# Delta rule with key products up to 15 chunks ahead, solved matrices through DRAM, and two moved pieces of work in the experts

## The chip, the cores and the metric

The kernel runs on one NeuronCore of a Trainium2 chip. Its five engines work side by side, each through its own instruction stream: PE (TensorE, matmuls; its weight loads are listed as PEld), DVE (VectorE), ACT (ScalarE), POOL (GpSimd) and SP (SyncE, which here only issues DMAs). The metric is the device time of one execution in microseconds (us), smaller is better. Before the change the median of three runs is 974.29 us (973.56 to 976.66).

## The reference

Three stages, one after the other, all in float32:

```
# 1. attention by the delta rule; q, k, v: [4 batches, 8 heads, 768 tokens, 48]
k_n = k / (norm(k) + 1e-06);  state = 0                       # 48 x 48 per head
for t in range(768):
    y[t]   = q[t] @ state
    v_old  = state applied to k_n[t]
    state += beta[t] * outer(k_n[t], v[t] - v_old)
# 2. mixture of experts: 3072 tokens of width 384, 8 experts, the best one each
e   = argmax(cosine(x, expert_emb) / tau)
out = gate * (relu(x @ w1[e]) @ w2[e])                         # 384 -> 1024 -> 384
# 3. dense feed-forward
h = relu(x @ w_in);  out = (h * h) @ w_out                     # 384 -> 2048 -> 384
```

## The kernel before

**The delta stage.** The 768 tokens are cut into 24 chunks of 32, and four chunks make a group (6 groups). Within a chunk the recurrence is turned into matrices, so that only the 48 x 48 states pass from chunk to chunk. For each chunk `gram` (lines 146 to 190) multiplies keys by keys and queries by keys (64 matmuls, line 154) and ACT copies the products to `GPs` and `Pm`. After the last chunk of a group from group 2 on, the products go to DRAM and come back laid out by lane: `GPs` to `gscr` (L176) and back as `AL` (L179), `Pm` to `pscr` (L184) and back as `PL2` (L188; `PL` in the rows). All four are DMAs that SP issues in order, so each waits for the one ahead of it.

`lanes` (lines 196 to 296) makes the list of DVE operations that solves a group's 128 triangular 32 x 32 systems at once, one per lane: 31 steps of a multiply into `tmp` (L269) and an add into `TL` (L277), with the scaling of `vV` (L259) and the masking of `PL` (L194) among the last steps. At the end four transposes on DVE (L282, `STREAM_TRANSPOSE`) turn the solved matrix `TL` into `TTt`, which PE reads in `W` (L343).

**The chunk loop** (from line 774) runs for each chunk: `mmV` and `mm1K` (PE, L301 and L313), `U` (L324 on DVE writes `Ub` from the PSUM tile `ch`), `W` (PE, L343, reads `Ub` and `TTt`; DVE and ACT then write `Wb`), one `gram` for a chunk further on, the router's logits of the chunk before (`xlog`), the state update `dS` (L362) and the output `PW` (L394). So from chunk to chunk DVE waits for PE at `Ub`, and PE waits for DVE at `W`. Which `gram` runs is set by `ahead` and its limit `min(15 if s < 4 else NS, s + 12)`: chunks 1 to 12 each run one of the grams 12 to 23.

**The planner.** The solving operations stand in streams, one per group, and `fill(now, part)` pops them into DVE's program three times per chunk: a cost in us is attached to each (`0.1 + n / 960`), `need` works out the pace at which every group would be done at its due time `due(g) = 4 * g` (the chunk of its first use), and `fill` pops as much as the pace allows. The order is fixed when the kernel is built; nothing of it is decided on the chip.

**The experts** (`moe`) run eight times: 8 blocks of the first product (line 1121 and on, tiles `gp`, `sp`, `yp`, `xp`; `hh` and `hl` are the high and the low part of the activation), and then the second product. The leftover 64 rows of an expert use `ht` (L1184, tile `t2k`), which DVE writes after the last block and PE waits for at L1208. Meanwhile DVE prepares the weights of stage 3: `w64` splits each of 28 pieces (lines 1058 to 1092) into parts that are stored to `wscr` and fetched back (L602). `run(k, ng, nw)` after each block pops `ng` gate operations and `nw` of these, two per block in the last expert. At the end PE places the last rows with one-hot matrices (`t2k` of L1245, matmuls of L926), POOL scatters rows into `x` in DRAM (L1216).

**The dense stage** is 8 blocks of 384 tokens, PE-bound. `load_x2(n + 1)` (lines 1130 to 1135) reads the rows of the next block from `x` and stands at the start of each block, the first included, ahead of some of the fetches of `W<-wscr` on SP.

Of the kernel before, what the change touches and what calls it, by code (L numbers as in the profile page):

```python
# [8 lines left out]
F32 = mybir.dt.float32  # L9
# [12 lines left out]
def kernel(  # L22
# [16 lines left out]
    nc = tc.nc  # L39
# [3 lines left out]
    NS, C = kq.shape[0], kq.shape[-1]  # L43
    S = NS * C
    E, _, FF = moe_w1.shape
# [13 lines left out]
    cp = pool("const")  # L59
# [3 lines left out]
    wscr = [dram.tile([128, 6144], F32, name=f"wscr{i}") for i in range(2)]  # L63
    pscr = [dram.tile([4, C, 4, 256], F32, name=f"pscr{i}") for i in range(2)]
    gscr = [dram.tile([4, C, C, C], F32, name=f"gscr{i}") for i in range(2)]

    ident = cp.tile([128, 128], F32, name="ident")
    magic = cp.tile([128, C], I32, name="magic")
# [40 lines left out]
    gp = apool("gp")  # L109
# [15 lines left out]

    def load_kq(s):
        if s % 3 == 0:
            KQ3[0] = cp.tile([128, 3, 4, 4, 2, C], F32, name="W", bufs=5)
        a = KQ3[0][:, s % 3]
        KQ[s] = a[:, :, :, 0], a[:, :, :, 1], a  # L130
        nc.sync.dma_start(a, kq[s])
# [14 lines left out]
    def gram(s, n0=0, n1=2, banks=GP2):  # L146

        g, i = divmod(s, 4)
        n = n1 - n0
        for p in range(4):  # L150
            for h2 in range(2):
                for b in range(4):
                    r = 64 * h2
                    PE.matmul(
                        banks[h2][C * b : C * b + C, p * n * C : (p + 1) * n * C],
                        KQ[s][0][r : r + 64, p, b],
                        KQ[s][n0][r : r + 64, p, b]
                        if n == 1
                        else KQ[s][2][r : r + 64, p, b].rearrange("d n j -> d (n j)"),
                        start=True,  # L160
                        stop=True,
                    )
        if i == 0 and n0 == 0:
            GPs[g] = gp.tile([128, 4, 8, C], F32, name="GPs", bufs=3)
        if i == 0 and n1 == 2:
            Pm[g] = gp.tile([128, 4, 4, 2, C], F32, name="Pm", bufs=3)
        for m in range(n0, n1):
            for h2 in range(2):
                if m == 0:
                    o = GPs[g][:, i].rearrange("p (x a c) j -> p c x a j", x=2, c=2)[:, h2]  # L170
                else:
                    o = Pm[g][:, :, i].rearrange("p (a c) x j -> p c x a j", c=2)[:, h2]
                src = banks[h2][:, : 128 * n].rearrange("p (x a n j) -> p n x a j", x=2, a=2, n=n)
                A.activation(o, src[:, m - n0], AF.Copy)
        if i == 3 and n0 == 0 and g > 1:
            nc.sync.dma_start(gscr[g % 2].rearrange("b i u j -> (b i) (u j)"), GPs[g].rearrange("p s h j -> p (s h j)"))  # L176
            ALs[g] = wp.tile([128, C, C], F32, name="AL", bufs=3)
            for b in range(4):
                nc.sync.dma_start(ALs[g][C * b : C * b + C], gscr[g % 2][b].rearrange("i u j -> u i j"))  # L179
        if i == 3 and n1 == 2:  # L180
            scr = pscr[g % 2]
            PL2[g] = gp.tile([128, 4, 4, 2, C], F32, name="PL2", bufs=4)
            for b in range(4):
                nc.sync.dma_start(  # L184
                    scr[:, :, b, :].rearrange("f j x -> j f x"),
                    Pm[g][C * b : C * b + C].rearrange("p f s c j -> p f (s c j)"),
                )
            nc.sync.dma_start(  # L188
                PL2[g].rearrange("p b s c j -> p (b s c j)"), scr.rearrange("f j b x -> (f j) (b x)")
            )  # L190
# [5 lines left out]
    def lanes(g):  # L196
# [82 lines left out]
        def end(i):  # L279
# [3 lines left out]
                TTl[g].rearrange("p u i -> p i u")[:, i : i + 8], T.rearrange("p c i -> p i c")[:, i : i + 8]  # L283
            )

        for j in range(31):
            for f in (mul, acc):
                add(lambda f=f, j=j: f(j), (31 - j) * (j + 1))
            if j in (23, 25, 27, 29):
                u = (j - 23) // 2  # L290
                add(lambda u=u: vh(u), 384)
                if g:
                    add(lambda u=u: masked(g, u), 256)
        for i in range(0, C, 8):
            add(lambda i=i: end(i), c=0.55)
        return ops

    def mmV(s, hq):

# [235 lines left out]
    def padding(e):  # L535

        o = xs[e * CAP : (e + 1) * CAP] if e < E else x2[0:384]
        n = 112 if e < E else 128
        nc.scalar.dma_start(
            o.rearrange("(a p) c -> p a c", p=n),  # L540
            pad[:n, : o.shape[1]].unsqueeze(1).broadcast_to([n, o.shape[0] // n, o.shape[1]]),
        )
# [96 lines left out]
        V.tensor_tensor(lo, raw1[a], hi.bitcast(F32), ALU.subtract)  # L639

    def attention():
        streams, route_q = deque(), deque()
        budget, lent = 0.0, 0.0

        class Stream:
# [6 lines left out]
            def pop(self):  # L652
                c, f = self.ops.popleft()
                f()
                self.left -= c
                if not self.ops:
                    streams.remove(self)
                return c

        def need(now):  # L660
# [33 lines left out]
                budget = 0.0  # L694

        def due(g):
            return 4 * g

        def queue(fs):
            route_q.extend(fs)  # L700
# [70 lines left out]
        for s in range(NS):  # L771
            g, i = divmod(s, 4)
            last = g == NG - 1
            while s not in ready:
                streams[0].pop()
            if s:
                mmV(s, 0)
                mmV(s, 1)
                mm1K(s, 0)
                mm1K(s, 1)  # L780
            U(s)
            fill(s, 0.25)
            if s:
                mm1Q(s)
            if s > 0:
                xT = xrt(s - 1)
            while streams and streams[0].g <= g:
                streams[0].pop()
            W(s, 0)
            W(s, 1)  # L790
            if s == NS - 1:
                lows.pop(0)()
            if s == 0:
                for b in range(4):
                    masked(0, b)
            if ahead < min(15 if s < 4 else NS, s + 12):
                gram(ahead)
                ahead += 1
            if scats and s >= E:
                drain(route_q)  # L800
                scats.pop(0)()
            fill(s + 0.25, 0.4)
            if s == NS - 4:
                first_x()
            if s >= NS - 3:
                pre1(s - NS + 3, False)
            if scats and s >= NS - 10:
                scats.pop(0)()
            if R is not None and s in (6, 10, 14, 17, 19):
                drain(route_q)  # L810
                R[1]()
                queue(R[2])
                scats += R[3]
            if s > 0:
                xlog(s - 1, xT)
                if i == 0 or s == 18:
                    R = route(g, 0, 2) if i else route(g - 1, 2 if s == 20 else 0, 4)
                    R[0][0]()
                    queue(R[0][1:])
                    if last and i == 0:  # L820
                        drain(route_q)
            if s + 1 < NS:
                dS(s, 0)
                dS(s, 1)
            if s == NS - 1:
                R = route(NG - 1, 2, 3)
                for o in R[0]:
                    o()
            PW(s)
            if last and i == 0:  # L830
                R[1]()
                queue(R[2])
                scats += R[3]
            if s <= E:
                padding(s)
            if i == 3 and g + 2 < NG:
                load_v(g + 2)
                load_k2(g + 2)
            if s % 3 == 2:
                for n in range(s + 13, min(s + 16, NS)):  # L840
                    load_kq(n)
            if ahead % 4 == 0 and ahead // 4 - 1 > made:
                made += 1
                streams.append(Stream(made, s + 1.6))
            fill(s + 0.65, 0.35)
            if s in (15, 17, 20):
                pre1((15, 17, 20).index(s), True)
            if s in (NS - 3, NS - 2):
                R = route(g, s - NS + 3, s - NS + 4)
                for o in R[0] + [R[1]] + R[2]:  # L850
                    o()
                scats += R[3]
# [241 lines left out]
    def moe():  # L1094
# [48 lines left out]
        for e in range(E):  # L1143
# [21 lines left out]
            for fb in range(8):  # L1165
# [11 lines left out]
                if fb == 3 and e + 1 < E:  # L1177
                    load_x(e + 1)
                if e:
                    run(fb + 1, 4, 2 if e + 1 == E else (1, 1, 0, 1, 0, 1, 0, 1)[fb])  # L1180
                else:
                    run(fb + 1, (0, 0, 0, 0, 2, 4, 6, 9)[fb], 1)
            ht = mp.tile([128, 8, 64], F32, name="t2k", bufs=2)
# [66 lines left out]
        for o in late:  # L1250
            o()
        for n in range(NBLK):
            if n + 1 < NBLK:
                load_x2(n + 1)
            xhn, xln = xh[f"a{n}"], xl[f"a{n}"]
            sh, sl = [
# [4 lines left out]
            for fb in range(16):  # L1261
# [13 lines left out]
                def part2(fb=fb, s2=s2, sh=sh, sl=sl):  # L1275
                    A.activation(sh[fb], s2, AF.Copy)
                    V.tensor_tensor(sl[fb], s2, sh[fb].bitcast(F32), ALU.subtract)

                if n == 0:
                    weights(10 * E + 2 + (fb + 1) * 8 // 15)  # L1280
            part2()
# [76 lines left out]
```

## Time and profile before

| | us |
|---|---|
| median of 3 runs | 974.29 (973.56 to 976.66) |
| the profiled execution | 973.39 |
| its span | 971.6 |
| PE busy in it | 908.7 (94%) |
| DVE busy in it | 620.7 (64%) |
| ACT busy in it | 443.6 (46%) |

The profile shows one execution. Start times count from the beginning of its span. The delta stage lies between 49 and 268 us, the first expert's start follows, the experts run to 556 us, the dense stage to the end. The mean clock that TensorE was granted over the span is 0.951 of the full one. A row of a timeline gives start, duration, engine, line, operation, the tile written and the tile read, a count, and in brackets the idle time before it with the instruction that ended it.

### The profile page before, as it was taken

The page shows a single profiled execution, that of the slowest core. Times are in us where ns is not written, and L with a number is a line of the kernel's source. Part 1 is how long each engine was busy: PE and PEld are TensorE (multiplying, and loading weights), DVE is VectorE, ACT ScalarE, POOL GpSimd, SP SyncE. Part 2 cuts the span into 40 slices and gives each one's busy share as a digit, 9 for nine tenths or more (in the row PEclk, how much of TensorE's full clock was granted, in tenths as well). Part 3 has the DMA queues.
Part 4 walks back from the last instruction along what each step waited for, and adds up shares of the span by engine and source line. Part 5 has one row for each costly group of instructions (what it writes and reads, how often), then busy time and mean ns, then how long its engine had stood idle before and what let it go on. Part 6 is the DMA issues. An engine that isn't in the chain of part 4 may idle for free. (4 is left out here: it accounts for less than half of the span.)

```text
span 971.6 us, 22202 instructions
## 1 busy us (share of the span) xinstructions
PE 908.7 (94%) x8982; PEld 810.4 (83%) x8982; DVE 620.7 (64%) x1641; ACT 443.6 (46%) x1051; POOL 89.4 (9%) x126
## 2 busy tenths in 40 slices
PE   4778889899999999999999899999999999999998
PEld 3456667677777798888887689999999999999998
DVE  7999997899667888888789572423334241516060
ACT  2247656557734555455555362423333242415150
POOL 2000012011211122212211200000000000000000
PEclk7579988789989999999999999999999999999999
DMA  8667865441145677477557450101010101010000
GB/s 322 204 186 230 251 172 191 102 144 58 65 142 187 214 245 243 133 245 252 175 181 241 147 163 17 33 9 42 9 41 9 41 9 41 1 49 1 25 1 25
DMA packets 70608, 117.75 MB, mean 121 GB/s; under 512 B 22659, under 2 KB 48746, under 8 KB 70496
## 3 DMA queue, kind: packets, MB, share of 16 engines
q1 hardware_dynamic: 60784, 94.08, 30.4%
q0 software_dynamic: 5440, 15.88, 4.3%
q10 hardware_dynamic: 4272, 6.28, 2.0%
q8 instruction: 72, 1.18, 0.5%
q14 instruction: 40, 0.33, 0.1%
HBM read 84.12 MB, written 32.89 MB: 120 GB/s over the span
## 5 line engine op out<-in xcount | busy, mean ns | idle before, releaser
L1272 DVE TENSOR_TENSOR t4k<-t2k 128x384 f32<-128x384 f32 x128 | 71.4, 558 | 231.9 <-ACT t2k L1271 231.3
L277 DVE TENSOR_TENSOR TL<-TL,tmp 128x31 f32<-128x31 f32 (+15 forms) x186 | 62.7, 340 | 3.6
L269 DVE TENSOR_TENSOR tmp<-AL,TL 128x31 f32<-128x31 f32 (+15 forms) x186 | 62.4, 339 | 3.3
L1121 PE MATMUL gp<-wb,hh 128*128 128x384 f32 x184 | 62.9, 342 | 0.0
L1123 PE MATMUL gp<-wb,hl 128*128 128x384 f32 x184 | 62.0, 337 | 0.6 <-DVE hl L1174 0.6
L1122 PE MATMUL gp<-wb,hh 128*128 128x384 f32 x184 | 61.8, 336 | 0.0
L372 ACT ACTIVATE Sb<-sp 48x384 f32<-48x384 f32 x92 | 44.6, 484 | 34.0 <-PE sp L362 32.5
L1121 PE MATMUL sp<-xh,W 128*128 128x384 f32 (+1 forms) x150 | 51.0, 340 | 2.2 <-ACT t2k L1271 2.2
L1122 PE MATMUL yp<-xl,W 128*128 128x384 f32 (+1 forms) x153 | 52.6, 344 | 0.1
L1121 PE MATMUL yp<-xh,W 128*128 128x384 f32 (+1 forms) x153 | 52.5, 343 | 0.2 <-ACT xh L950 0.2
L1123 PE MATMUL yp<-xh,W 128*128 128x384 f32 (+1 forms) x153 | 52.6, 344 | 0.0
L1123 PE MATMUL gp<-xh,W 128*128 128x384 f32 (+1 forms) x153 | 52.1, 340 | 0.0
L1121 PE MATMUL gp<-xh,W 128*128 128x384 f32 (+1 forms) x153 | 52.0, 340 | 0.0
L1122 PE MATMUL gp<-xl,W 128*128 128x384 f32 (+1 forms) x153 | 51.9, 340 | 0.0
L362 PE MATMUL sp<-Wb,kL 128*48 128x96 f32 x736 | 49.5, 291 | 2.3 <-issue 1.4
L1121 PE MATMUL xp<-wb,hh 128*128 128x384 f32 x152 | 51.3, 338 | 0.0
L1123 PE MATMUL sp<-xh,W 128*128 128x384 f32 (+1 forms) x150 | 51.2, 341 | 0.0
L1123 PE MATMUL xp<-wb,hl 128*128 128x384 f32 x152 | 51.1, 336 | 0.0
L1122 PE MATMUL xp<-wb,hh 128*128 128x384 f32 x152 | 51.1, 336 | 0.0
L1122 PE MATMUL sp<-xl,W 128*128 128x384 f32 (+1 forms) x150 | 50.9, 340 | 0.0
L1216 POOL DMA_INDIRECT x<-y,rows x32 | 35.4, 1105 | 127.2 <-ACT y L1213 72.6
L362 PEld LDWEIGHTS sp<-Wb,kL 128*48 128x48 f32 x736 | 41.7, 149 | 6.0 <-ACT Wb L356 2.6
(314 smaller groups left out, 2463.7 us busy)
## 6 DMA issues: line engine op xcount, KB each, us to landing
W<-in_moe_w_dram SPq DMA_DIRECT2D x42, 256.0 KB, 3.6
W<-in_kq_dram SPq DMA_DIRECT2D x20, 512.0 KB, 7.0
hb<-in_moe_w_dram SPq DMA_DIRECT2D x24, 384.0 KB, 3.3
t4k<-in_moe_w_in_dram SPq DMA_DIRECT2D x12, 512.0 KB, 4.2
t4k<-in_moe_w_out_dram SPq DMA_DIRECT2D x16, 384.0 KB, 3.7
W<-wscr SPq DMA_DIRECT2D x16, 384.0 KB, 4.1
xs<-padrow ACTq DMA_DIRECT2D x8, 693.0 KB, 5.1
xe<-xs SPq DMA_DIRECT2D x8, 594.0 KB, 8.3
```

What stands on the lines that cost most here:

```text
L269: V.tensor_tensor(tv[0], AL[:, j, j + 1 :].unsqueeze(1).broadcast_to([128, n, m]), T[:, :n, j : j + 1].broadcast_to([128, n, m]), ALU.mult,)
L277: V.tensor_tensor(T[:, : j + 1, j + 1 :], T[:, : j + 1, j + 1 :], tv[0], ALU.add)
L362: PE.matmul(SP_[hq][64 * par : 64 * par + D, b * 96 : b * 96 + 96], kL2[g][:, i, b * 2 + hq], Wb[hq].rearrange("p b (m r) e -> p b r m e", ...
L372: A.activation(Sb[hq][r : r + D, :, :, par, :], SP_[hq][r : r + D, 0:384].rearrange("p (b m e) -> p b m e", b=4, m=2), AF.Copy,)
L1121: PE.matmul(ps, hs, rh, start=first, stop=False)
L1122: PE.matmul(ps, hs, rl, start=False, stop=False)
L1123: PE.matmul(ps, ls, rh, start=False, stop=last)
L1216: to_x2 = lambda n=n, t=t, y=y, rows_e=rows_e: G.indirect_dma_start(out=x2, out_offset=bass.IndirectOffsetOnAxis(ap=rows_e[:n, t : t + 1]. ...
L1272: V.tensor_tensor(s2, r, r, ALU.mult)
```

## The change

- The solved matrices of groups 2 to 5 are no longer transposed on DVE. When such a group's stream ends, `stored` writes `TL` to a DRAM tile `tscr` (one DMA on SP), and `relaid` reads it back with rows and columns exchanged into `TTt` (four DMAs on SP). `relaid` is called at the end of a chunk, from chunk 4g - 5 on, or at the latest ahead of `W`.
- These groups are due at 4g - 2.2 instead of 4g.
- Two grams may run in a chunk from chunk 2 on, and the limit of `ahead` is 15, 18 or s + 15. The grams run in chunks 0 (12), 1 (13), 2 (14), 3 (15, 16), 4 (17, 18), 5 (19) and so on to 9 (23).
- The keys and queries of chunks 15 to 17 are loaded in chunk 0 into a buffer of their own, and each later load comes three chunks earlier; `GPs` and `Pm` have two buffers instead of three.
- In the last expert 2, 2, 2, 2, 2, 2, 0, 0 of the `w64` operations are popped after the eight blocks instead of two after each.
- `load_x2(1)` stands after the tenth of the 16 parts of dense block 0 instead of at its start.

```
+    tscr = [dram.tile([4, C, C, C], F32, name=f"tscr{i}") for i in range(2)]
...
-            KQ3[0] = cp.tile([128, 3, 4, 4, 2, C], F32, name="W", bufs=5)
+            KQ3[0] = (wp if s == 15 else cp).tile([128, 3, 4, 4, 2, C], F32, name="W", bufs=1 if s == 15 else 5)
...
-            GPs[g] = gp.tile([128, 4, 8, C], F32, name="GPs", bufs=3)
+            GPs[g] = gp.tile([128, 4, 8, C], F32, name="GPs", bufs=2)
...
+        def stored():
+            nc.sync.dma_start(tscr[g % 2].rearrange("b u c i -> (b u) (c i)"), T.rearrange("p c i -> p (c i)"))
...
-        for i in range(0, C, 8):
+        if g > 1:
+            ops.append((0.0, stored))
+        for i in range(0, C if g < 2 else 0, 8):
             add(lambda i=i: end(i), c=0.55)
         return ops
+
+    def relaid(g):
+
+        TTl[g] = wp.tile([128, C, C], F32, name="TTt", bufs=2)
+        for b in range(4):
+            nc.sync.dma_start(TTl[g][C * b : C * b + C], tscr[g % 2][b].rearrange("u c i -> c u i"))
...
         def due(g):
-            return 4 * g
+            return 4 * g - (2.2 if g > 1 else 0)
...
+            if g not in TTl:
+                solved.remove(g)
+                relaid(g)
             W(s, 0)
...
-            if ahead < min(15 if s < 4 else NS, s + 12):
-                gram(ahead)
-                ahead += 1
+            for _ in range(2 if s > 1 else 1):
+                if ahead < min(15 if s < 3 else 18 if s < 4 else NS, s + 15):
+                    gram(ahead)
+                    ahead += 1
...
+            if s == 0:
+                for n in range(15, 18):
+                    load_kq(n)
...
-                for n in range(s + 13, min(s + 16, NS)):
+                for n in range(s + 16, min(s + 19, NS)):
...
+            old = list(solved)
             fill(s + 0.65, 0.35)
+            for x in old:
+                if s >= 4 * x - 5:
+                    solved.remove(x)
+                    relaid(x)
...
-                    run(fb + 1, 4, 2 if e + 1 == E else (1, 1, 0, 1, 0, 1, 0, 1)[fb])
+                    run(fb + 1, 4, ((1, 1, 0, 1, 0, 1, 0, 1), (2, 2, 2, 2, 2, 2, 0, 0))[e + 1 == E][fb])
...
-            if n + 1 < NBLK:
+            if 0 < n < NBLK - 1:
                 load_x2(n + 1)
...
+                if n == 0 and fb == 9:
+                    load_x2(1)
```

Three places of the program show the moves. The first is SP, from the load of `vV` for group 2 on, before the change; the buffers' numbers tell neighbouring groups apart.

```order
L140 DMA vV<-in_v_dram 128x1536
L144 DMA kL_1602<-in_k_dram 128x1536
L176 DMA gscr_67<-GPs 128x1024
L179 DMA AL<-gscr_67 32x32x32 x4
L184 DMA pscr_65<-Pm 32x4x256 x4
L188 DMA PL_1719<-pscr_65 128x1024
L131 DMA W<-in_kq_dram 128x1024 x3
L140 DMA vV<-in_v_dram 128x1536
```

The same stretch of SP after the change (the old line numbers are up to 28 higher there).

```order
L177 DMA gscr_67<-GPs 128x1024
L180 DMA AL<-gscr_67 32x32x32 x4
L185 DMA pscr_65<-Pm 32x4x256 x4
L189 DMA PL_1603<-pscr_65 128x1024
L141 DMA vV<-in_v_dram 128x1536
L145 DMA kL_1695<-in_k_dram 128x1536
L177 DMA gscr_66<-GPs 128x1024
L180 DMA AL<-gscr_66 32x32x32 x4
L185 DMA pscr_64<-Pm 32x4x256 x4
L189 DMA PL_2029<-pscr_64 128x1024
L132 DMA W<-in_kq_dram 128x1024 x3
L288 DMA tscr_68<-TL 128x1024
```

The round trip of group 3 (`gscr_67`, `pscr_65`) now stands ahead of the load of `vV` for group 2, and that of group 4 (`gscr_66`, `pscr_64`) and a load of keys stand ahead of the store of group 2's solved matrix; the four reads of it follow right behind.

The second place is DVE where group 2's solve ends. Before, this is in chunk 6, behind that chunk's `Ub`; the `sm` operations between belong to the next group's norms.

```order
L324 TENSOR_TENSOR Ub_109<-ch_101,blk 128x768
L259 TENSOR_TENSOR vV<-vV,sm 128x384
L85 SCALAR_TENSOR_TENSOR sm<-sm 128x32
L194 TENSOR_TENSOR PL_841<-PL_841,mask 128x256
L82 TENSOR_TENSOR sm<-sm 128x32
L269 TENSOR_TENSOR tmp_1990<-AL,TL 128x31
L84 SCALAR_TENSOR_TENSOR sm<-sm 128x32
L277 TENSOR_TENSOR TL<-TL,tmp_1990 128x31
L85 SCALAR_TENSOR_TENSOR sm<-sm 128x32
L324 TENSOR_TENSOR Wb_112<-ch_102,blk 128x768
L282 STREAM_TRANSPOSE TTt<-TL 128x8x32
```

After the change it ends ahead of the same chunk's `Ub`.

```order
L260 TENSOR_TENSOR vV<-vV,sm 128x384
L195 TENSOR_TENSOR PL_843<-PL_843,mask 128x256
L86 SCALAR_TENSOR_TENSOR sm<-sm 128x32
L270 TENSOR_TENSOR tmp_2099<-AL,TL 128x31
L91 TENSOR_TENSOR sm<-sm 128x32
L278 TENSOR_TENSOR TL<-TL,tmp_2099 128x31
L92 TENSOR_SCALAR sm<-sm 128x32
L336 TENSOR_TENSOR Ub_111<-ch_103,blk 128x768
```

The last step moved ahead of `Ub` of chunk 6, and no transpose follows.

The third is SP at the end of the experts, from the last fetches of one half of the dense weights (`wscr_62`) to those of the other (`wscr_63`), before the change.

```order
L602 DMA W<-wscr_62 128x768 x2
L1135 DMA xe<-x_61 128x384 x3
L602 DMA W<-wscr_62 128x768 x2
L1135 DMA xe<-x_61 128x3x384
L602 DMA W<-wscr_63 128x768 x8
```

And after it.

```order
L614 DMA W<-wscr_62 128x768
L1161 DMA xe<-x_61 128x384 x3
L614 DMA W<-wscr_62 128x768 x2
L614 DMA W<-wscr_63 128x768 x6
L1161 DMA xe<-x_61 128x3x384
L614 DMA W<-wscr_63 128x768 x2
```

The rows of dense block 1 (`xe<-x_61 128x3x384`) moved behind six of the eight fetches of `wscr_63`.

## Rows read from the trace of the kernel before

**Rows 1.** Windows: us, busy PE, PEld, DVE, ACT, POOL, clock, DMA share, GB/s
```profile
81.63:210.44 128.81, 111.81 (x2515) 85.64 (x2515) 116.39 (x377) 78.36 (x222) 14.73 (x18) 0.88 0.58 175
210.44:240.47 30.03, 28.76 (x548) 21.82 (x552) 28.30 (x90) 20.64 (x53) 5.52 (x7) 0.94 0.23 85
240.47:262.29 21.82, 21.58 (x444) 15.94 (x436) 12.54 (x55) 16.40 (x43) 5.69 (x8) 1.00 0.15 57
```
**Rows 2.** Lines of DVE from 81.63 to 210.44: busy us, mean ns | idle before
```profile
L277 DVE TENSOR_TENSOR TL<-TL,tmp 128x135 f32<-128x135 f32 (+15 forms) x100 | 34.3, 343 | 2.5
...
L324 DVE TENSOR_TENSOR Ub<-ch,blk 128x768 f32<-128x768 f32 x13 | 12.4, 952 | 7.8 <-PE ch L313 7.8
L282 DVE STREAM_TRANSPOSE TTt<-TL 128x256 f32<-128x256 f32 x13 | 8.3, 657 | 0.0
L259 DVE TENSOR_TENSOR vV<-vV,sm 128x384 f32<-128x384 f32 x12 | 6.6, 551 | 0.0
L194 DVE TENSOR_TENSOR PL<-PL,mask 128x256 f32<-128x256 f32 x12 | 5.0, 416 | 0.0
```
**Rows 3.** Timeline of DVE, `Ub` of chunks 5, 10, 11 and 13
```profile
100.70 0.95 DVE L324 TENSOR_TENSOR Ub<-ch,blk 128x768 f32<-128x768 f32 x1
...
150.12 0.96 DVE L324 TENSOR_TENSOR Ub<-ch,blk 128x768 f32<-128x768 f32 x1 [2.10 <-PE ch L313]
...
160.95 0.96 DVE L324 TENSOR_TENSOR Ub<-ch,blk 128x768 f32<-128x768 f32 x1 [2.28 <-PE ch L313]
...
183.45 0.96 DVE L324 TENSOR_TENSOR Ub<-ch,blk 128x768 f32<-128x768 f32 x1 [2.27 <-PE ch L313]
```
**Rows 4.** Timeline of PE: `W` of chunk 8, grams of chunks 10 and 12
```profile
130.59 0.94 PE L343 MATMUL ch<-Ub,TTt 128*32 128x192 f32 x16
...
152.25 0.86 PE L154 MATMUL gp<-W 64*32 64x64 f32 x64
...
173.57 1.11 PE L154 MATMUL gp<-W 64*32 64x64 f32 x42
174.98 0.68 PE L154 MATMUL gp<-W 64*32 64x64 f32 x22 [0.29 <-issue]
```
**Rows 5.** Timeline of SP in chunks 4 to 6, a group's round trip
```profile
94.15 0.33 SPq L176 DMA_DIRECT2D gscr<-GPs  x1
...
109.20 2.35 SPq L131 DMA_DIRECT2D W<-in_kq_dram  x3
```
**Rows 6.** DMA issues from 40 to 270: KB each, us from issue to landing
```profile
AL<-gscr SPq DMA_DIRECT2D x16, 128.0 KB, 3.8
pscr<-Pm SPq DMA_DIRECT2D x16, 128.0 KB, 3.0
```
**Rows 7.** Timeline of DVE and PE at the last expert's end
```profile
537.05 0.69 DVE L1184 TENSOR_TENSOR t2k<-hh,hl 128x512 f32<-128x512 f32 x1 [1.66 <-DMA wscr<-t2k]
...
537.79 2.79 PE L1208 MATMUL xp<-hb,t2k 128*64 128x384 f32 x8 [3.82 <-DVE t2k L1184]
...
551.31 0.42 DVE L1245 TENSOR_SCALAR t2k<-t4k,xe 128x384 fp32r<-128x384 int32 x1 [2.58 <-DMA wscr<-t2k]
...
552.25 0.61 PE L926 MATMUL ch<-t2k,t4k 128*128 128x384 f32 x2 [0.93 <-DVE t4k L1230]
```
**Rows 8.** Timeline of POOL, SP, ACT and PE at the start of the dense stage
```profile
558.07 1.00 POOL L1216 DMA_INDIRECT x<-y,rows  x1 [4.10 <-issue]
...
561.15 18.64 SPq L602 DMA_DIRECT2D W<-wscr  x8
...
565.75 0.84 ACT L576 ACTIVATE wb<-W 128x768 fp32r<-128x768 f32 x1 [4.38 <-DMA W<-wscr]
...
567.02 0.45 PE L1121 MATMUL sp<-xh,W 128*128 128x384 f32 x1 [2.15 <-ACT t2k L1271]
```
**Rows 9.** Windows of 4 us behind the two waits (columns as in Rows 1)
```profile
540.00:544.00 4.00, 4.00 (x20) 2.41 (x17) 2.25 (x6) 1.64 (x3) 0.73 (x2) 0.84 0.35 134
568.00:572.00 4.00, 4.00 (x15) 4.00 (x15) 3.79 (x8) 3.40 (x7) 0.00 (x0) 0.57 0.45 117
```

More of the change, by code (lines that the diff above doesn't have):

```diff
@@ L163, in gram @@
         if i == 0 and n0 == 0:
-            GPs[g] = gp.tile([128, 4, 8, C], F32, name="GPs", bufs=3)
+            GPs[g] = gp.tile([128, 4, 8, C], F32, name="GPs", bufs=2)
         if i == 0 and n1 == 2:
-            Pm[g] = gp.tile([128, 4, 4, 2, C], F32, name="Pm", bufs=3)
+            Pm[g] = gp.tile([128, 4, 4, 2, C], F32, name="Pm", bufs=2)
         for m in range(n0, n1):
@@ L641, in attention @@
     def attention():
-        streams, route_q = deque(), deque()
+        streams, route_q, solved = deque(), deque(), deque()
         budget, lent = 0.0, 0.0
@@ L657, in pop @@
                     streams.remove(self)
+                    if self.g > 1:
+                        solved.append(self.g)
                 return c
@@ L839, in attention @@
             if s % 3 == 2:
-                for n in range(s + 13, min(s + 16, NS)):
+                for n in range(s + 16, min(s + 19, NS)):
                     load_kq(n)
-            if ahead % 4 == 0 and ahead // 4 - 1 > made:
+            while ahead // 4 - 1 > made:
                 made += 1
                 streams.append(Stream(made, s + 1.6))
+            old = list(solved)
             fill(s + 0.65, 0.35)
+            for x in old:
+                if s >= 4 * x - 5:
+                    solved.remove(x)
+                    relaid(x)
             if s in (15, 17, 20):
```

## Prediction, made before the changed kernel ran

> **What bounds the kernel now.** I read the windows by stage first, then the lines and waits of the engine that each window shows as full, and last the timelines around the longest waits. In the dense stage PE is full, and the change leaves its matmuls as they are. In chunks 3 to 15 no engine is full: DVE works 116.39 of 128.81 us, PE 111.81 at a granted clock of 0.88 [rows 1]. The two hand work to each other in each chunk, DVE being the longer: of its 12.42 us of idle time 7.8 stand before `Ub`, where it waits for PE, the rest in small gaps [rows 2]. Those waits lie late: chunk 5 has none, chunks 10, 11 and 13 have 2.10, 2.28 and 2.27 [rows 3]. In chunks 16 to 19 DVE still solves and fills 28.30 of 30.03, or 7.51 per chunk; in chunks 20 to 22 it solves nothing, works 12.54 of 21.82, and a chunk takes 7.27, PE's own length [rows 1]. At the experts' end and the start of the dense stage two PE waits stand out, 3.82 and 2.15 [rows 7, 8].
>
> **Solving on DVE, chunks 3 to 15.** I counted operations in the two programs between the `Ub` of chunk 3 and that of chunk 16. Transposes fall from 13 to 1: 12 x 0.657 = -7.9. The earlier due times bring in 25 more multiplies and adds, one `vV` and one mask. A step of the solve costs 0.343, and the 2.5 idle before 100 of them adds 0.025 [rows 2]: 25 x 0.368 = +9.2; the other two add 0.551 + 0.416 = +1.0. Net +2.3 of DVE. Three of the 13 chunks have a wait of over 2 at `Ub` that can take their share: -0.5. If all of it fell into waits it would cost 0, if none +2.3. I take +1.8.
>
> **Chunks 16 to 19.** They lose those operations and 4 transposes, some 12.8 us of DVE's 28.30. Then PE is late next, as in chunks 20 to 22: 4 x 7.27 = 29.1 against 30.03, -0.9. The gain can't pass that, since PE's work stays; without it, 0.
>
> **Key products.** Chunks 10, 11 and 12 have no `gram` any more. It stands on PE between `W` and the work that leads to the next `Ub`. In chunk 10 it took 0.86; in chunk 12 it took from 173.57 to 175.66, 2.09, its rows being longer there and broken by 0.29 [rows 4]. Both stand ahead of a `Ub` that waits longer than this (chunks 11 and 13, 2.28 and 2.27 [rows 3]): -3.0. Chunk 11's gram stands before a `Ub` without a long wait and gives nothing. Bounds: 0, and -4.6 if these two waits go altogether. In chunks 3 and 4 two more grams run, 2 x 0.86 = 1.7 of PE and eight copies on ACT, at a time when DVE does not wait for PE. Between 0 and +1.7 I take the middle, +0.9.
>
> **The way through DRAM.** DVE's transposes become DMAs, and SP's order decides their time. The `vV` of group 2 now stands behind the round trip of group 3. From `gscr` to the load of keys that ends the trip SP took 109.20 - 94.15 = 15.05 [rows 5]. With the gram that starts it in chunk 2 or 3 instead of 4, I work out landing at 100.7 to 103.8, and DVE's first use near the end of chunk 4, at about 100.7 [rows 3]: a wait of 0 to 2.6, taken +0.5. Queued behind an instruction on DVE that waits here are the rest of the solve and then `Ub` of chunk 5, for which PE waits.
>
> The store of group 2's solved matrix waits behind group 4's round trip. That starts with the gram of chunk 5, say at 104 (its `Ub` is at 100.70 [rows 3]); with 15.05 for the trip and 2.35 to issue the keys [rows 5] the store is issued at 121.5. The reads fetch 512 KB in 128-byte pieces, as `AL<-gscr` does, which lands 3.8 after its issue; the store has 3.0 or so [rows 6]. With the waits of one DMA for another and their issue that is 127 to 136, against `W` of chunk 8 at 130.59 [rows 4], some 1 us later by the terms above. So 0 to +5, at worst +14.5 (two long trips behind each other); I take +0.5. Later groups have 4 to 14 us more, from the same sum, and cost nothing.
>
> [...]
>
> **The experts.** (a) PE waits 3.82 for `ht`, which DVE writes at 537.05 [rows 7]. Popping four operations fewer ahead of it (0.42 each, as the one element-wise row of this stretch, L1245 [rows 7]) and without the store that ended the 1.66 of idle time, `ht` comes 1.7 + 4 x 0.42 = 3.4 earlier, PE saves 3.4 there. But the four operations now follow `ht`, and what ends this part is `t2k` of L1245 at 551.31, itself waiting 2.58 for a store of these pieces [rows 7]. I let it, and with it the matmul at 552.25, come 2.1 earlier, since DVE is busy only 2.25 of 4 us behind `ht` [rows 9]. PE, done earlier, then idles 3 to 4 longer before that matmul. After such waits the clock falls: 0.84 in the 4 us behind the first wait, 0.57 in those behind the one at 567.02 [rows 9]. I charge 1.1 for it, between (1 - 0.84) x 4 = 0.6 and (1 - 0.57) x 4 = 1.7. Net -1.0; bounds -5 (both waits and their clock) and +0.5.
>
> (b) The rows for dense block 1 can be read only after the scatter at 558.07, and the eight fetches of `wscr` stand behind them: issued at 561.15, they let ACT wait 4.38 until 565.75, and PE 2.15 until 567.02 [rows 8]. With six fetches ahead of the rows, both waits go. If PE's clock stays up behind, the 1.7 of the last row goes too: -2.15 to -3.85. Something else may keep PE waiting (0). I take -3.6, near the far end, since a fetch issued when the scatter is still to come has over 4 us of room. The rows themselves are needed at the end of block 0, tens of us later.
>
> **The sum.** +1.8 - 0.9 - 3.0 + 0.9 + 0.5 + 0.5 = -0.2 in the delta stage, -4.6 in the experts: -4.8. From the profiled execution's 973.39 that gives 968.6. It lies 0.9 under the median of the runs, so on the median's scale I predict 969.5.
>
> **Rivals.** *All waits at `Ub` go.* The change spreads PE's work so evenly that DVE runs through. For it: PE has 17 us of room in 128.81, and the grams now come early, where no `Ub` waits. Against it: the waits lie where PE runs at a low clock, and nothing in the change touches chunks 8 and 9. The 7.8 goes instead of the 3.0 + 0.5 counted (-4.3), and the three charges of 0.9, 0.5 and 0.5 with it (-1.9): 969.5 - 6.2 = 963.3.
>
> *The solve moved forward shows in full.* DVE is the longer engine, the waits stay where they are, chunks 16 to 19 gain nothing. +2.3 + 0.9 + 0.5 + 0.5 = +4.2, with (b) alone of the experts' -3.6: +0.6, 974.9. For it: chunks 3 to 7, where most of the work arrives, show no waits to fill. Against it: the three grams that vanish.
>
> *Slower: group 2's matrices come late to `W` of chunk 8.* PE then stands, and behind it `dS`, `PW` and the next `Ub`; the place is the four reads behind group 4's trip on SP. It makes the kernel slower from landings of some 8 us after the need (140 instead of 132), since 4.8 must be used up and 2.9 passed. Long waits in SP's queue speak for it (4 to 15 us per trip [rows 5]), the margins worked out above against it. With 11 us of lateness: 969.5 - 0.5 + 11 = 980. [...]
>
> **How the numbers follow.** A measurement of this kernel can tell a change of about 0.3%, 2.9 us: faster is under 971.4, slower above 977.2. The sum as forecast has 0.47 (own range 964 to 972.5; a tenth of it within 0.3%), all waits going 0.20, the solve in full 0.20 (three quarters of it within 0.3%), late matrices 0.08 (a quarter within), a larger gain than any of these 0.05. Faster 0.42 + 0.20 + 0.05 = 0.67; the same 0.05 + 0.15 + 0.02 = 0.22; slower 0.11. The range of 960 to 977 takes in the first three cases and leaves out most of the last two.
>
> **What would show it.** In the changed kernel's windows DVE's busy time between the same two `Ub` should be some 1 to 3 us more and the stretch about as long; chunks 16 to 19 should come to 29.1. The waits before `Ub` of chunks 11 and 13 should be under 1.5. `W` of chunk 8 should start without a long wait on a DMA, and the first `vV` operation of group 2 too. The wait for `ht` should be under 1, that of the low part's placement longer than 0.93. The first matmuls of the dense stage should not wait for ACT, and the 4 us behind them should be at full clock. The forecast is wrong if the delta stage differs by more than 4 us either way, or if the wait at 567.02 is still there.

## The result and the profile after

The changed kernel takes 981.86 us (median; 979.09 to 983.61) against 973.56 for the kernel before on the same chip: a ratio of 1.0088, 95% interval 1.0062 to 1.0114. It is 8.3 us slower, where 4.8 less was forecast. The profiled execution took 980.09, its span is 978.0, against 973.39 and 971.6 before.

The loss lies in the delta stage. `Ub` of chunk 23 starts at 272.95 instead of 262.29, 10.7 later; from there to the end 705.1 us are left instead of 709.3, so the experts gain 4.3. Windows of the changed kernel (columns as in Rows 1; chunks 3 to 15, 16 to 19, 3 to 8, 9 to 15, then chunks 4, 5 and 8 by themselves):

```profile
81.84:222.58 140.74, 117.22 (x2447) 89.91 (x2440) 118.28 (x393) 77.48 (x218) 15.02 (x18) 0.82 0.61 169
222.58:251.19 28.61, 28.50 (x583) 21.12 (x577) 16.97 (x59) 21.48 (x56) 4.14 (x6) 1.00 0.49 136
81.84:157.69 75.85, 59.58 (x1356) 45.87 (x1349) 56.15 (x190) 38.65 (x116) 4.69 (x7) 0.77 0.66 190
157.69:222.58 64.89, 57.63 (x1103) 44.04 (x1095) 62.13 (x204) 38.83 (x102) 10.33 (x12) 0.87 0.54 145
92.51:108.68 16.17, 11.30 (x316) 8.75 (x304) 10.39 (x33) 8.71 (x27) 0.00 (x0) 0.89 0.77 217
108.68:119.71 11.03, 10.02 (x170) 7.67 (x174) 8.89 (x36) 4.50 (x13) 0.00 (x0) 0.55 0.59 158
141.21:157.69 16.48, 10.96 (x217) 8.30 (x209) 9.03 (x34) 6.27 (x18) 3.57 (x6) 0.69 0.72 197
```

The kernel before, chunks 3 to 8, 9 to 15, and chunks 4, 5 and 8:

```profile
81.63:139.40 57.77, 48.88 (x1244) 37.89 (x1244) 54.40 (x170) 37.89 (x109) 2.64 (x4) 0.94 0.68 208
139.40:210.44 71.04, 62.94 (x1271) 47.75 (x1271) 61.99 (x209) 40.47 (x113) 12.09 (x14) 0.83 0.51 148
90.69:100.70 10.01, 9.00 (x205) 7.19 (x205) 9.67 (x30) 5.64 (x17) 0.00 (x0) 0.83 0.54 173
100.70:109.03 8.33, 7.41 (x205) 5.93 (x205) 8.12 (x28) 6.05 (x19) 0.00 (x0) 1.00 0.89 206
129.33:139.40 10.07, 8.78 (x252) 6.69 (x240) 9.73 (x30) 7.93 (x23) 1.69 (x3) 1.00 0.69 223
```

Against [rows 1], chunks 3 to 15 take 11.9 us more, but DVE works only 1.9 more in them: 10 us are new idle time. Chunks 3 to 8 lose 18.1, and chunks 9 to 15 win 6.1 back. Chunk 4 loses 6.2 and chunk 8 loses 6.4, each with a stall in it, and chunk 5, behind the first stall, loses 2.7. Chunks 5 and 8 run with PE at a granted clock of 0.55 and 0.69. The lines of DVE in chunks 3 to 15, against [rows 2] (idle before each and what ended it behind the second bar), and the waits of PE there (us in total, times, longest):

```profile
L278 DVE TENSOR_TENSOR TL<-TL,tmp 128x135 f32<-128x135 f32 (+15 forms) x113 | 39.1, 348 | 2.0
...
L336 DVE TENSOR_TENSOR Ub<-ch,blk 128x768 f32<-128x768 f32 x14 | 13.4, 956 | 7.0 <-PE ch L325 7.0
L336 DVE TENSOR_TENSOR Wb<-ch,blk 128x768 f32<-128x768 f32 x13 | 12.3, 948 | 5.8 <-ACT Wb L368 5.8
L260 DVE TENSOR_TENSOR vV<-vV,sm 128x384 f32<-128x384 f32 x13 | 7.1, 550 | 5.4 <-DMA vV<-in_v_dram 5.4
```
```profile
PE ch L355 <- DVE Ub L336: 13.4, 7, 4.8
PE ch L355 <- DMA TTt<-tscr: 5.5, 1, 5.5
PE gp L155 <- ACT Pm L175: 2.1, 2, 1.1
PE gp L155 <- DMA W<-in_kq_dram: 1.8, 1, 1.8
```

Three transfers are late: `vV` of group 2 (DVE waits 5.40 in chunk 4), `TTt` of group 2 (PE waits 5.5 at chunk 8, and DVE's 5.8 at `Wb` is the same wait seen from behind) and the keys of chunks 21 to 23 (1.8). SP's timeline shows why, against [rows 5]:

```profile
85.33 0.33 SPq L177 DMA_DIRECT2D gscr<-GPs  x1
...
101.23 0.35 SPq L141 DMA_DIRECT2D vV<-in_v_dram  x1
...
112.75 0.33 SPq L177 DMA_DIRECT2D gscr<-GPs  x1
...
126.21 8.35 SPq L132 DMA_DIRECT2D W<-in_kq_dram  x3
134.65 0.38 SPq L288 DMA_DIRECT2D tscr<-TL  x1
140.92 3.83 SPq L308 DMA_DIRECT2D TTt<-tscr  x4
```

`vV` stands behind the round trip of group 3, which takes 15.9 us, and is issued at 101.23; before the change its load was ahead of that trip. Its use on DVE, and what PE does after it and after the wait for `TTt`:

```profile
108.00 0.56 DVE L260 TENSOR_TENSOR vV<-vV,sm 128x384 f32<-128x384 f32 x1 [5.40 <-DMA vV<-in_v_dram]
```
```profile
109.69 1.51 PE L355 MATMUL ch<-Ub,TTt 128*32 128x192 f32 x16 [4.81 <-DVE Ub L336]
...
148.06 1.51 PE L355 MATMUL ch<-Ub,TTt 128*32 128x192 f32 x16 [5.52 <-DMA TTt<-tscr]
```

`W` takes 1.51 behind either stall instead of 0.94 [rows 4]: PE comes back at the lower of its clock's two levels (1.2 of 2.4 GHz), as these windows show, and the work that follows takes longer by that as well:

```profile
108.68:118.00 9.32, 8.31 (x135) 6.19 (x136) 8.89 (x35) 4.08 (x13) 0.00 (x0) 0.50 0.50 154
148.06:156.00 7.94, 7.94 (x134) 6.03 (x134) 6.20 (x26) 4.00 (x12) 1.00 (x1) 0.50 0.57 211
```

The landing times in this stretch (DMA issues from 40 to 270, as [rows 6]) are longer than those of before for `vV`, and `TTt` is no slower than its neighbours. The first line is of the kernel before, the others of the changed kernel:

```profile
vV<-in_v_dram SPq DMA_DIRECT2D x5, 768.0 KB, 4.3
```
```profile
vV<-in_v_dram SPq DMA_DIRECT2D x5, 768.0 KB, 6.8
...
pscr<-Pm SPq DMA_DIRECT2D x16, 128.0 KB, 4.2
tscr<-TL SPq DMA_DIRECT2D x4, 512.0 KB, 4.9
TTt<-tscr SPq DMA_DIRECT2D x16, 128.0 KB, 4.1
```

The Trainium skill ("VectorE: DVE Perf Modes", section "The three transpose paths") calls a plain DMA copy that transposes by its strides 19 times slower than a transposing DMA when the innermost stride of the destination is large. Here the reads keep runs of 128 bytes whole on both sides, so that condition isn't met, and no run here tests it. The transposing reads land in 4.1. They are late by their place in the queue.

The experts, against [rows 7, 8] (waits of PE from 500 to 600): the 3.82 is 1.3, the 2.15 at the start of the dense stage is gone, and two waits of 1.9 and 1.7 stand before the placement of the last rows instead of 0.93. So the wait that the pops took away ahead of `ht` (2.5) came back ahead of the last rows (2.7).

```profile
PE ch L952 <- DVE t4k L1256: 1.9, 1, 1.9
PE ch L952 <- ACT y L1239: 1.7, 1, 1.7
PE xp L1234 <- DVE t2k L1210: 1.3, 1, 1.3
```

### The profile page after: what moved, and what is told of

Same layout as the page of the kernel before. It is cut to its first block, busy times and chain, and to the rows that moved or that the text cites. A ratio compares the mean times of both kernels' runs of the same rounds, so it can differ in the third digit from the quotient of the medians.

```text
span 978.0 us, 22229 instructions
## 1 busy us (share of the span) xinstructions
PE 909.6 (93%) x8982; PEld 813.1 (83%) x8982; DVE 611.5 (63%) x1625; ACT 443.5 (45%) x1051; POOL 88.7 (9%) x126
## 5 line engine op out<-in xcount | busy, mean ns | idle before, releaser
L278 DVE TENSOR_TENSOR TL<-TL,tmp 128x87 f32<-128x87 f32 (+15 forms) x186 | 62.3, 339 | 2.9
L270 DVE TENSOR_TENSOR tmp<-AL,TL 128x87 f32<-128x87 f32 (+15 forms) x186 | 62.2, 339 | 3.0
L355 PE MATMUL ch<-Ub,TTt 128*32 128x192 f32 x384 | 24.5, 368 | 26.0 <-DVE Ub L336 20.4
```

The lines of the kernel that those rows point to most:

```text
L270: V.tensor_tensor(tv[0], AL[:, j, j + 1 :].unsqueeze(1).broadcast_to([128, n, m]), T[:, :n, j : j + 1].broadcast_to([128, n, m]), ALU.mult,)
L278: V.tensor_tensor(T[:, : j + 1, j + 1 :], T[:, : j + 1, j + 1 :], tv[0], ALU.add)
L355: PE.matmul(CH[hq][C * f : C * f + C, 256:448], TTl[g][:, i * 8 + hq * 4 + f], Ub[hq][:, f].rearrange("p b e -> p (b e)"), start=True, sto ...
```

## The experiments

Times are medians of the runs of each kernel, ratios are to the kernel before in the same session, which had 973.1 to 974.0; the waits are those of one profiled execution. E below is the kernel before with the experts' two edits.

**First, which part is slower.** T stands for late transfers, R for the price of the work moved forward.

The load of `vV` ahead of the gram:

```
+            if i == 3 and g + 2 < NG:
+                load_v(g + 2)
             for _ in range(2 if s > 1 else 1):
```

> The changed kernel with the load of vV moved ahead of the chunk's gram (and so ahead of the round trip that this gram starts on SP). Theory T (two transfers come late through SP's queue, and PE's low clock behind each stall adds to it): the wait of 5.40 on DVE for vV goes, and with it most of the 2.7 by which chunk 5 is longer; the wait of 5.52 for TTt at chunk 8 stays, since the chain ahead of it moves earlier together with the need. Time 8 us less than the changed kernel, 973 to 975. Rival R (the solve moved forward and the double grams cost the time, and the waits only stand where DVE would work anyway): 1 to 2 us less, about 980.

Measured: 979.09, ratio 1.0055 (1.0033 to 1.0076); 2.8 less than the changed kernel, though the two intervals overlap. The profiled execution, at 973.0, is the shortest of the twelve. In it the wait for `vV` is gone, but PE waits 4.5 for the keys at chunk 7 instead of 1.8, and chunk 7 takes 14.5. One late transfer gave way to the next.

The transposes back on DVE:

```
-        if g > 1:
-            ops.append((0.0, stored))
-        for i in range(0, C if g < 2 else 0, 8):
+        for i in range(0, C, 8):
```

> The changed kernel with the four DVE transposes back for every group, nothing through tscr; due times, key products and experts as changed. T: no wait for TTt at chunk 8, chunk 8 falls from 16.5 to about 10 us; 16 transposes of 0.66 come back on DVE (10.5), about half of them in waits: 2 us less than the changed kernel, 979 to 981. R: 5 us more than the changed kernel (986 to 987), as DVE has more to do.

Measured: 982.53 (1.0048 to 1.0111), the same as the changed kernel. Chunk 8 fell to 9.5, but `vV` is waited for 6.0, and DVE works 6.2 more in chunks 3 to 15 (124.50 against 118.28). Here the late way through DRAM and the transposes on DVE cost the same.

Both together:

> Both of the above: neither vV nor TTt late. T: 9 to 11 us less than the changed kernel, 971 to 973, the gain of the experts (about 4) plus nothing in the delta stage. R: 983 to 985.

Measured: 981.03 (1.0042 to 1.0086). Neither `vV` nor `TTt` is late, the keys are (3.4), and it is no faster. T as stated falls: without the two stalls there is no gain, with the transposes' work back on DVE (124.4 busy in chunks 3 to 15, against 118.3 in the changed kernel and 116.4 before).

The experts' edits on the kernel before (E):

> The kernel before with the experts' two edits alone (the 2, 2, 2, 2, 2, 2, 0, 0 pops and load_x2(1) moved). T and R: about 4.2 us less than before, 969 to 970, as the changed kernel's trace gains 4.2 from chunk 23 to the end. If the gain in that trace came from elsewhere (the clock's state on entering the experts): within 1.5 us of before.

Measured: 969.98, ratio 0.9964 (0.9942 to 0.9986), 3.6 less than before. And `load_x2(1)` moved alone:

> The kernel before with load_x2(1) moved alone. By the prediction's split: 3.6 less than before and 1.0 more than both of the experts' edits. By the clock's share alone (2.15): 2.2 less than before.

Measured: 970.42, 0.9975 (0.9953 to 0.9997), 2.7 less. So most of the gain is the moved load; for the pops about 0.9 is left, too little to tell from none. (The 2.15 in this expectation is the wait of [rows 8], not a share of the clock.)

**Taking all three loads out of SP's way.** `vV` and keys ahead of the gram, store and reads of `tscr` on POOL's queue (`nc.gpsimd.dma_start`):

> The changed kernel with three transfers taken out of the round trips' way on SP: vV and the keys and queries of three chunks ahead are loaded before the chunk's gram, and the store and reads of the solved matrices go through POOL's queue. T (three transfers late through SP's order: vV at chunk 5, keys at chunk 7, TTt at chunk 8, each with low clock behind it): no wait of PE or DVE on a DMA in chunks 3 to 15; 968 to 972. R (the early grams and the solve moved forward cost the time by themselves): 977 or more, with chunks 3 to 8 still at 10 to 12 us each.

Measured: 989.58 (1.0127 to 1.0213), slower than all. With the keys ahead of group 4's trip, DVE waits 8.6 for `AL` in chunk 6. Chunk 20 takes 15.8, as PE waits 5.6 for the last `TTt`, which is now issued on the queue that also scatters rows. The same with `tscr` on SP:

> As the kernel above, but the solved matrices stay on SP. T: the store still waits behind group 4's round trip, so W of chunk 8 waits 2 to 5 us for TTt and the clock falls behind: 3 to 6 us above the kernel above. If TTt is late only because everything ahead of it was: the same time as the kernel above.

Measured: 975.46 (1.0006 to 1.0050). `TTt` is not waited for here, so T's form of this expectation failed; `AL` is, for 4.1. This is the changed kernel with nothing but the place of two kinds of loads changed, and it is 6.4 faster than it (5.8 by the ratios): about that much of the loss was the order on SP. With the earlier due times one transfer or another comes late in either order.

**The parts one at a time, on E.** The key products alone (`due` back to `4 * g`, transposes on DVE):

> The kernel before with the experts' edits and the key products alone (early grams, earlier loads; due times 4g, DVE transposes). T: the keys of chunks 21 to 23 come late at chunk 7 (3 to 5 us and the clock behind), vV in time since the solve is not moved: 972 to 976 against 970 for the experts' edits alone. R in its form that the double grams cost by themselves: chunks 3 and 4 longer by 2 to 4 us together. If neither: 966 to 969.

Measured: 966.58 (0.9874 to 0.9938), 3.4 less than E, although PE waits 8.4 for the keys at chunk 7 in the profiled execution, which is the longest of the ten (956.52 to 969.06):

```profile
PE gp L155 <- DMA W<-in_kq_dram: 8.4, 1, 8.4
```

The due times and the way through DRAM, with the grams as before:

> The kernel before with the experts' edits, the due times 2.2 chunks earlier and the way through DRAM, but the grams as before. T: SP's round trips start as late as before, so vV and TTt are in time and the solve moved forward costs about 1 net of what it saves in chunks 16 to 19: 969 to 972. R in its form that the solve moved forward costs by itself: 976 or more.

Measured: 975.37 (1.0009 to 1.0054), 5.4 more than E, with no wait of PE or DVE on a DMA above 0.5. DVE is busy 124.33 in chunks 3 to 15, 7.9 more than in [rows 1]:

```profile
82.41:216.21 133.80, 112.01 (x2515) 86.91 (x2515) 124.33 (x390) 79.48 (x223) 13.93 (x17) 0.87 0.69 194
```

The due times alone, transposes on DVE:

> The kernel before with the experts' edits and the due times 2.2 chunks earlier alone (grams as before, DVE transposes). If the due times cost by themselves (theory D, from the run of due times with the way through DRAM: 5.4 above the experts' edits, with no wait on a DMA): 974 to 977. If that cost came from the way through DRAM (its traffic, SP's queue): 969 to 972.

Measured: 979.35 (1.0041 to 1.0096), 9.4 more than E. The due times are the costly part, and the way through DRAM takes 4.0 of it back. Part of the cost lies in chunks 16 to 19, which take 33.77 instead of 30.03 [rows 1]: the rest of the solve and its transposes now end in chunks 16 and 17, which grow to 10.00 and 9.35, while chunks 18 and 19, at 7.2 each, win nothing back.

```profile
216.53:250.30 33.77, 30.02 (x549) 22.42 (x552) 23.54 (x76) 20.78 (x53) 5.90 (x8) 0.90 0.23 84
```

With the key products, 4g - 1.1:

```
-            return 4 * g - (2.2 if g > 1 else 0)
+            return 4 * g - (1.1 if g > 1 else 0)
```

> The experts' edits and the key products (966.6 with due times 4g, 982.5 with due times 4g - 2.2), here with due times 4g - 1.1. D, as a cost in proportion to the lead: about 974. If the cost sets in only where a transfer becomes late (vV for group 2 first needed ahead of 108): 966 to 970, with DVE waiting under 3 us for vV or AL.

Measured: 978.09, ratio 1.0058 (1.0031 to 1.0085): 11.5 more than with 4g, above both expectations. Half the lead costs most of the 16.0 between 4g and 4g - 2.2 (966.58 and 982.53): the keys are waited for 9.7, `AL` 2.7. It is no cost in proportion, nor one with a safe margin.

**Why the due times cost without a late transfer.** With them alone, DVE's busy time in chunks 3 to 15 is 126.42 against 116.39 [rows 1], 10 more, of which 7 more pairs of steps explain 6.0 (all multiplies and adds last 74.4 instead of 68.4). The window, then two stretches of DVE's timeline:

```profile
81.37:216.53 135.16, 115.12 (x2515) 88.98 (x2515) 126.42 (x391) 78.68 (x221) 15.20 (x18) 0.85 0.55 166
```
```profile
105.23 0.29 DVE L270 TENSOR_TENSOR tmp<-AL,TL 128x135 f32<-128x135 f32 x1
105.56 0.30 DVE L278 TENSOR_TENSOR TL<-TL,tmp 128x135 f32<-128x135 f32 x1
105.89 0.28 DVE L270 TENSOR_TENSOR tmp<-AL,TL 128x112 f32<-128x112 f32 x1
...
113.00 0.19 DVE L83 TENSOR_TENSOR sm<-sm 128x32 f32<-128x32 f32 x1
113.23 0.19 DVE L85 SCALAR_TENSOR_TENSOR sm<-sm 128x32 f32<-128x32 f32 x1
113.45 0.19 DVE L86 SCALAR_TENSOR_TENSOR sm<-sm 128x32 f32<-128x32 f32 x1
```

One group's steps stand alone, and the next group's small operations stand alone behind them, each 0.22 to 0.23 after the one that it needs. In the fastest version, below, they stand between each other:

```profile
112.16 0.29 DVE L270 TENSOR_TENSOR tmp<-AL,TL 128x135 f32<-128x135 f32 x1
112.37 0.18 DVE L232 TENSOR_TENSOR sm<-sm,betaL 128x32 f32<-128x32 f32 x1
112.48 0.30 DVE L278 TENSOR_TENSOR TL<-TL,tmp 128x135 f32<-128x135 f32 x1
112.70 0.18 DVE L233 TENSOR_SCALAR sm<-sm 128x32 f32<-128x32 f32 x1
112.82 0.27 DVE L270 TENSOR_TENSOR tmp<-AL,TL 128x112 f32<-128x112 f32 x1
```

The same pair of steps takes 0.66 from multiply to multiply, with two small operations in it; alone it took 105.89 - 105.23 = 0.66. An operation that needs nothing of its neighbour starts 0.08 before that one's end, where a dependent one starts 0.04 behind it, so the two that stand between were free. The planner causes the difference: `fill` draws in an operation of the next group only with the time that the first group's due time leaves, and an earlier due time leaves less. Of the multiplies in chunks 3 to 15, 72 of 100 stand directly ahead of their add before the change, 79 of 107 with the due times alone (and 48 of 57 small operations of the norms behind another, none before), 36 of 100 with the key products alone, 63 of 112 in the changed kernel. To test it, the fastest version with DVE made to finish one group before the next:

```
-                    a, b = streams[0], streams[1] if len(streams) > 1 else None
+                    a, b = streams[0], None
```

> As the fastest version (experts' edits, key products, due times 4g, vV and keys loaded first: 957.0), but DVE finishes one group's solve before it starts the next: of 100 multiplies in chunks 3 to 15, 84 instead of 36 stand directly ahead of the add that needs them, and 32 instead of none of 57 small operations stand behind another of their chain. No due time and no transfer is changed. If the earlier due times cost because they take the other work out from between dependent operations: DVE's busy time in chunks 3 to 15 rises from 108 to about 116 to 118, and the time is 964 to 968. If they cost for another reason (the lead itself): 957 to 959.

Measured: 975.90, 18.9 more than the fastest version, with no wait on a DMA. DVE is busy 121.20 in its chunks 3 to 15, against 108.30 in the fastest version:

```profile
86.04:215.86 129.82, 110.80 (x2451) 86.25 (x2451) 121.20 (x381) 77.86 (x218) 13.92 (x17) 0.87 0.52 155
```
```profile
83.29:201.40 118.11, 105.63 (x2419) 81.63 (x2421) 108.30 (x378) 77.06 (x216) 16.65 (x17) 0.91 0.57 172
```

The direction is as expected and the size larger. Busy time counts an instant once, so it is the sum of the single durations less their overlap. Added up over DVE's operations that start in chunks 3 to 15 (us, from the traces):

| | durations | overlap | busy |
|---|---|---|---|
| before | 135.1 | 18.7 | 116.4 |
| E, due times alone | 142.2 | 15.8 | 126.4 |
| E, due times and way through DRAM | 138.3 | 14.0 | 124.3 |
| changed kernel | 139.0 | 20.7 | 118.3 |
| fastest version | 135.8 | 27.5 | 108.3 |
| the same, one group after the other | 136.5 | 15.3 | 121.2 |

In the last two rows the work is the same to 0.7, and 12.2 of the 12.9 between their busy times is overlap. With the due times alone the loss of overlap is 2.9 of 10, and 7.1 is more work in this stretch: there order is the smaller part. A run with the earlier due times and the overlap given back was not made. The profiled executions differ by 15.6 in their spans (972.4 and 956.8): 11.7 in these chunks, 2.8 ahead of chunk 3.

**The fastest version.** E with the key products, due times 4g, transposes on DVE, `vV` and keys ahead of the gram:

```
+            if i == 3 and g + 2 < NG:
+                load_v(g + 2)
+            if s % 3 == 2:
+                for n in range(s + 16, min(s + 19, NS)):
+                    load_kq(n)
             for _ in range(2 if s > 1 else 1):
```

> The experts' edits and the key products with due times 4g and DVE transposes, and with vV and the keys loaded ahead of the chunk's gram. If the wait of 8.4 for the keys at chunk 7 and that of 1.6 for vV are lost time (theory T): chunk 7 falls from 18.1 to 10 or 11 us, 958 to 961. If they stand where PE has to wait for the solve anyway: 965 to 968.

Measured: 956.98, ratio 0.9838 (0.9809 to 0.9867), 16.1 less than before; chunk 7 falls from 18.1 to 9.6. The same with one gram per chunk:

> As the fastest version, but one gram per chunk (chunks 0 to 11 run grams 12 to 23), so no gram waits for ACT's copies of another in chunks 3 and 4. If the double grams cost by themselves: chunk 3 falls from 12.3 to 9 us and the time is 954 to 956. If the lead that they give is worth more (group 3's products one chunk earlier, 36 instead of 48 multiplies directly ahead of their add): 960 to 963.

Measured: 959.53 (0.9828 to 0.9880). Chunk 3 falls from 12.3 to 11.2 only. The median is 2.6 higher, but by the ratios to the kernel before it is 1.6, and the intervals overlap: that the second gram per chunk is worth its price is likely, not shown.

## Why the prediction was wrong

- **The failed step: the two waits under the way through DRAM, put at 0.5 each.** The places were right, `vV` of group 2 and `TTt` at chunk 8, but 5.4 and 5.5 came, and the low clock behind them made chunk 5 longer as well (11.0 instead of 8.3). For `vV` the sum had a landing at 100.7 to 103.8; it was issued only at 101.23 and took 6.8, to 108.0. The store of the solved matrix was worked out from a gram at 104 and came from one at 112.75, mostly because of `vV`'s stall, and 8.35 instead of 2.35 went on issuing the keys; the store itself, sized by one of a quarter of its bytes (3.0), took 4.9. The chain needed each of its times to be right, while the wait taken from it was 0.5. The order on SP is shown as the cause of about 6 us: so much comes back when two kinds of loads alone are placed elsewhere. The slower rival named `TTt`'s half of this with a chance of 0.08 and gave 980 for 11 us of lateness; 5.5 came, and the rest of the loss came from elsewhere, so that its number lies near 981.9 by luck.
- **A transfer was overlooked.** The keys of chunks 21 to 23 stand in the same queue; PE waits 1.8 for them here, 8.4 with the key products alone.
- **A second step failed, hidden in the changed kernel: the solve on DVE, +2.3 of work and +1.8 of time.** The +1.9 measured (118.28 against 116.39) agrees by luck. The price per operation holds only while its neighbours stay. With the due times and the way through DRAM, but the grams as before, the same count of operations costs DVE 7.9, of which 4.7 is lost overlap, and the stretch takes 133.80 instead of 128.81, with no transfer late. The early grams, which bring the next group's operations sooner, gave overlap back in the changed kernel. With the loads in time they take 8.1 of DVE's busy time away with no step fewer (108.30).
- **Chunks 16 to 19, 29.1:** 28.61, right.
- **Key products, -2.1 net:** chunks 11 and 13 have no wait left at `Ub`, as the step said, and chunks 9 to 15 take 64.9 instead of 71.0; two grams in chunk 3 and in chunk 4 made PE wait 1.0 each for ACT. Alone they gain 3.4 on E, and 13.0 with their loads in time, far above the -4.6 that bounded it: that bound knew only PE's side, and DVE's busy time falls as well.
- **The experts, -4.6:** 4.3 in the profile, 3.6 in the medians, right in sum. Of it 2.7 is the moved load (3.6 forecast, within the interval). For the pops -1.0 was forecast and 0.9 is left, which can't be told from none.
- **Of the other rivals**, "all waits go" is refuted here. "The solve moved forward shows in full" was priced at +4.2 for the delta stage (2.3 of it the solve), and the run nearest to it, the due times and the way through DRAM on E, has +5.4: of the rivals its mechanism is the one that the runs without a late transfer bear out.

What stays open: how the 11.9 of the changed kernel's chunks 3 to 15 divide between the stalls, the clock behind them and the solve moved forward. A run with the earlier due times, the early grams and every transfer in time was not reached: in each of four tries another transfer was late.

## What to carry to other kernels

A queue that issues in order has to be followed transfer by transfer, each with its need and the lateness that an earlier stall passes on; here a margin smaller than one landing time (4 to 7 us) was no margin. Dependent short operations on DVE want independent ones between them, as the run with one group after the other shows, so a planner that moves work forward should keep two streams running side by side. Before pulling a due time forward, check that its inputs arrive forward too.

## What the runs showed of the hardware

On DVE a dependent operation of 0.19 starts 0.22 to 0.23 after the one before, 0.04 behind its end, while an independent one starts 0.06 to 0.08 before the end of its predecessor (rows above). Over chunks 3 to 15 this made 12.2 of the 12.9 us by which DVE's busy time differs (121.20 against 108.30), with nearly the same operations in another order. Transposing reads from DRAM in 128-byte pieces landed in 4.1 for 128 KB, about as the 4.2 of the neighbouring stores.
